# A state-space mixer with an MLP gate: the first norm factors and two exponentials move from ScalarE to GpSimd, GELU's table is loaded first, and the work is put in another order

## The chip, the core and the metric

The kernel runs on one core of one Trainium2 chip. A core has a matrix engine (TensorE, PE in the profile; its weight loads are PEld) and three engines for elementwise work: VectorE (DVE), ScalarE (ACT) and GpSimd (POOL). SyncE (SP) issues most transfers; ScalarE and GpSimd can issue transfers from queues of their own. Each engine works through its own list of instructions in order, and waits on semaphores where an instruction needs what another engine makes. The metric is the device time of one execution, in microseconds (us).

## The reference

One input x of 2048 rows and 448 columns is normalised (the mean taken off, divided by the root of the variance). Two branches work on the normalised xn, and their product is added to x:

```python
xn = _layernorm(x, axis=-1)
# A: a linear recurrence over the rows, with 448 complex states
dt = jnp.exp(log_dt); Lam_bar = jnp.exp(dt * Lam)
B_bar = ((Lam_bar - 1.0) / Lam)[:, None] * Bmat
h = Lam_bar[None, :] * h + Bu[:, t, :]                  # for every row t
s = 2.0 * jnp.einsum("blp,dp->bld", hseq, Cmat).real + xn * Dskip
# B: an MLP on a second normalisation of xn, 448 -> 1792 -> 448
hid = _gelu(_layernorm(xn) @ w1 + b1)
g = _silu(hid @ w2 + b2)
out = x + s * g
```

Inputs and outputs are bf16. Lam is the complex vector Lambda, Bmat and Cmat are complex matrices.

## The kernel before, in words

The 2048 rows are four groups (0 to 3) of 512. A group has two blocks (b = 0, 1) of 256 rows, and of each block the even and the odd rows (par = 0, 1) are one tile of 128 rows and 448 columns. Rows lie on partitions. `x_all` holds x, `xn_sb` and `xn2_sb` the once and twice normalised rows, `xnT` and `xn2T` their transposes, which TensorE needs as operands. The later transposes are made by transfers; those of the first group's `xn2T` are made on TensorE (`first_apply`, line 460), and their results are copied out of PSUM at line 464 (the profile shows the helper's line, 417).

The MLP of a group has a first layer (`mm1_run`, line 801, matmuls over pairs j of 128 hidden columns, each pair in two phases, then GELU on ScalarE, line 805) and a second layer (`mm2`, line 828, 14 matmuls to a tile, then an eviction with the bias on VectorE, line 831, and SiLU or tanh on ScalarE). w1 has 448 rows: three transfers' worth of 128 and a rest of 64, which `ldw1` loads with a transfer of its own for each of four column chunks (lines 347 and 348, keys `w1_c` and `w1r_c`) and copies to a second place (line 352, `w1c_c`), so that two 64-row matmuls can run side by side.

The recurrence branch needs parameters first. `parameters()` turns the three vectors Lambda_re, Lambda_im and log_dt into columns with small matmuls (line 529), takes exp(log_dt) and exp(dt Lambda_re) (lines 533 and 541) and a sine and cosine of the angles by range reduction and a polynomial (lines 552 to 555, `wrap` and `sine`). `tables` builds rotation tables (lines 624 to 640), `lb` and `bt` the input matrix (lines 659 to 661, then transposes by transfer), `cq` the output matrices CQ and CZ, `m0` a direct term M0. Then, for every group, input matmuls (`bu`, line 729), the scan (`ssm`) and output matmuls (`ym`, lines 871 to 877), a product with the gate and a sum with x (lines 885 to 896).

The first group's statistics are read by `first_stats` (lines 431 and 432). The factor 1/sqrt(variance) is made on ScalarE: Ln, then Exp of minus a half (lines 434 and 435 for the two tiles of block 0, 438 and 439 for both tiles of block 1 at once). Ln and Exp share an activation table (`natural_log_exp_and_others`, loaded at line 314), GELU needs another, which `gelu_table` loads (line 443) once the last of these factors and of the exponentials is made. `ln_scale` (lines 478 to 488) makes later factors either on GpSimd by the power operation or on VectorE by Newton steps.

All of this is written down as tasks, numbered as they are created. A task names its engine, or two engines of which the list `SECOND` picks the second. The list `ORDER` is the order in which the tasks are given out; each engine gets its own tasks in that order and works through them in that order. Waits follow from what a task reads and writes. So the two lists set, for each queue, what stands behind what.

Until the first MLP matmul, TensorE runs filler matmuls (`dummies`, line 422) between the small ones. The order of the first tasks before the change is, on ScalarE: three loads of vectors, the first table, Ln and Exp of block 0, the parameter columns, exp(log_dt), two copies of transposes, Ln and Exp of block 1, the second exponential, the GELU table, GELUs. On VectorE: statistics and aggregate of one tile, then of the other, each followed soon by its normalising; the bias copy, the copies of w1, block 1. On SyncE: x of block 0 and 1, the w1 chunks with their rests, x of blocks 2 and 3, w2, the matrices.

## Time and profile before

| | us |
|---|---|
| median of 3 runs | 153.37 (153.15 to 153.41) |
| span of the profiled execution, first to last instruction | 151.8 |
| the runs' median less that span | 1.6 |
| first MLP matmul starts | 6.85 |
| last matmul ends | 148.91 |

| engine | busy us | share of the span |
|---|---|---|
| TensorE | 147.1 | 97% |
| VectorE | 127.6 | 84% |
| ScalarE | 99.0 | 65% |
| GpSimd | 42.1 | 28% |

The profile is one execution. Its rows give a start, a length, the engine, the line of the kernel, the operation, the output and the inputs with their shapes, and in brackets how long the engine was idle just before and whose work ended that wait. Matmuls are pipelined, so that a busy TensorE need not be at its peak. Lengths on GpSimd are rough.

### The profile page before, as it was taken

To read this page: it belongs to the slowest core of one execution; us is meant where nothing else is said; L and a number is where in the kernel's file an instruction comes from. 1 tells how busy PE (TensorE), PEld (TensorE's weight loads), DVE (VectorE), ACT (ScalarE), POOL (GpSimd) and SP (SyncE) were. 2 spreads that over 40 slices of the span, in tenths; PEclk is the share of its full clock that TensorE was granted. 3 is DMA by queue.
4 is the path that set the end of the run, shared out by engine and by line. 5 is a ranking of instruction groups with operands and counts; after the bars stand their busy time and mean duration, and the time that the engine had idled before them with its cause. 6 is when DMAs were issued, how large, how long until landed. Compare 5 with 4: busy or idle time off the path is not lost.

```text
span 151.8 us, 2974 instructions
## 1 busy us (share of the span) xinstructions
PE 147.1 (97%) x1127; PEld 86.6 (57%) x1127; DVE 127.6 (84%) x267; ACT 99.0 (65%) x183; POOL 42.1 (28%) x101
## 2 busy tenths in 40 slices
PE   7899999999999999999999999999999999999992
PEld 7785755454566577545444556764454666555551
DVE  2874999999978979999999996379968726999984
ACT  3888996988789559997898610463579834067400
POOL 5376827153020920010456006200072031000201
PEclk9999999999999999999999999999999999999999
DMA  4999999989997300700003032610331001100022
GB/s 116 262 305 390 266 202 138 219 152 133 165 261 180 65 0 0 138 0 4 0 0 63 4 60 45 154 60 4 60 101 23 0 4 57 64 0 0 4 84 98
DMA packets 31236, 14.73 MB, mean 97 GB/s; under 512 B 24752, under 2 KB 30774, under 8 KB 31222
## 3 DMA queue, kind: packets, MB, share of 16 engines
q1 hardware_dynamic: 30912, 14.26, 41.8%
q0 software_dynamic: 160, 0.23, 1.0%
q8 instruction: 9, 0.15, 0.4%
q10 hardware_dynamic: 150, 0.05, 0.1%
q14 instruction: 5, 0.04, 0.1%
HBM read 6.89 MB, written 1.84 MB: 57 GB/s over the span
## 4 chain that ended last, share of the span: by engine, by line
PE 80%; DVE 9%; DMA 4%; SPq 4%; issue 2%
PE psum L828 23%; PE psum L801 22%; PE psum L729 14%; PE psum L871 13%; DMA x_all<-in_A_x_dram 4%; PE psum L874 4%; SPq L84 4%; PE psum L712 3%; DVE xn_sb L499 2%; DVE lnst L399 1%; DVE s_w L628 1%; PE psum L877 1%; DVE o L831 1%; PE psum L697 1%; DVE tmp L891 1%
## 5 line engine op out<-in xcount | busy, mean ns | idle before, releaser
L801 PE MATMUL psum<-xn2T,w_sb 64*128 64x512 bf16 (+1 forms) x462 | 44.6, 345 | 0.3 <-ACT xn2T L417 0.2
L828 PE MATMUL psum<-w_sb,gT 128*128 128x448 bf16 x224 | 44.5, 353 | 0.2 <-DVE o L831 0.2
L805 ACT ACTIVATE gT<-psum,b1f 128x512 bf16<-128x512 f32 (+1 forms) x66 | 35.9, 625 | 10.4 <-PE psum L801 10.2
L801 PEld LDWEIGHTS psum<-xn2T,w_sb 64*128 64x128 bf16 x462 | 24.1, 109 | 19.8 <-ACT gT L805 2.3
L828 PEld LDWEIGHTS psum<-w_sb,gT 128*128 128x128 bf16 x224 | 21.5, 98 | 20.7 <-DVE o L831 0.6
L417 ACT ACTIVATE u_sb<-psum 128x512 bf16<-128x512 f32 (+2 forms) x22 | 10.5, 478 | 23.0 <-PE psum L729 22.7
L729 PE MATMUL psum<-xnT,BT 128*128 128x256 bf16 x196 | 24.0, 273 | 0.0
L729 PEld LDWEIGHTS psum<-xnT,BT 128*128 128x128 bf16 x196 | 18.9, 98 | 5.4 <-issue 1.1
L891 POOL TENSOR_TENSOR tmp<-t,x_all 128x448 bf16<-128x448 bf16 x5 | 5.2, 1032 | 33.1 <-DVE t L888 30.7
L753 DVE TENSOR_TENSOR_SCAN s_w<-dk,vs 128x774 f32<-128x774 f32 x8 | 14.0, 1760 | 0.1
L500 ACT ACTIVATE xn_sb<-x_all,lnw 128x448 bf16<-128x448 bf16 (+2 forms) x21 | 13.0, 662 | 1.2 <-DVE xn_sb L499 1.1
L417 ACT ACTIVATE vs<-s_w 64x256 bf16<-64x256 f32 (+2 forms) x16 | 10.9, 681 | 2.6 <-DVE s_w L753 1.5
L871 PE MATMUL psum<-CZ,h_sb 128*128 128x448 bf16 x56 | 11.9, 352 | 0.0
L871 PE MATMUL psum<-CQ,h_sb 128*128 128x448 bf16 (+2 forms) x54 | 10.5, 332 | 0.0
L399 DVE BATCH_NORM_STATS2 lnst<-x_all 128x6 f32<-128x448 bf16 x12 | 7.1, 617 | 3.4 <-DMA x_all<-in_A_x_dram 3.4
L831 DVE TENSOR_TENSOR o<-psum,b2bc 128x448 f32<-128x448 f32 x16 | 9.7, 614 | 0.2
L871 PEld LDWEIGHTS psum<-CZ,h_sb 128*128 128x128 bf16 x56 | 5.4, 98 | 4.7 <-DVE lnmv L405 0.4
L871 PEld LDWEIGHTS psum<-CQ,h_sb 128*128 128x128 bf16 x54 | 5.1, 98 | 4.0 <-DVE t L885 0.4
L874 PE MATMUL psum<-M,xnT 128*128 128x448 bf16 x32 | 7.4, 352 | 0.0
L480 POOL TENSOR_TENSOR lnw<-lnw,mhalf 128x8 f32<-128x8 f32 x3 | 7.2, 2404 | 0.3
L883 DVE TENSOR_TENSOR Cr<-psum,xd 128x448 f32<-128x448 f32 x7 | 4.3, 620 | 3.5 <-PE psum L877 3.4
L499 DVE TENSOR_SCALAR xn_sb<-x_all,lnw 128x448 bf16<-128x448 bf16 (+2 forms) x19 | 6.9, 396 | 0.0
(160 smaller groups left out, 189.1 us busy)
## 6 DMA issues: line engine op xcount, KB each, us to landing
out_dram<-tmp SPq DMA_DIRECT2D x7, 224.0 KB, 2.0
x_all<-in_A_x_dram SPq DMA_DIRECT2D x3, 448.0 KB, 4.0
w_sb<-in_B_w_dram SPq DMA_DIRECT2D x3, 448.0 KB, 8.4
w_sb<-in_B_w_dram SPq DMA_DIRECT2D x3, 384.0 KB, 4.8
vs<-in_A_C_re_dram SPq DMA_DIRECT2D x1, 392.0 KB, 11.6
Bn<-in_A_B_im_dram SPq DMA_DIRECT2D x1, 336.0 KB, 10.2
Bn<-in_A_B_re_dram SPq DMA_DIRECT2D x1, 336.0 KB, 10.5
vs<-in_A_C_im_dram SPq DMA_DIRECT2D x1, 336.0 KB, 10.8
```

Source lines behind the costliest of these rows:

```text
L399: dve([lambda e, b=b, par=par, q=q: e.bn_stats(lnst[:, q, :], x_all[:, 2 * g + b, par, :])], [f"x{2 * g + b}"] , [f"st{q}"], 0.62, prio)
L417: kb.either(("act", [lambda e, o=o, i=i: e.activation(o, i, ACT.Copy) for o, i in pairs]), ("dve", [lambda e, o=o, i=i: e.tensor_copy(o, i ...
L499: on = [("dve", [lambda e, o=o, i=i: e.tensor_scalar(o, i, rs, nb, op0=ALU.mult, op1=ALU.add) for o, i in parts], 0.4, 0.12), ("act", [lam ...
L500: ("act", [lambda e, o=o, i=i: e.activation(o, i, ACT.Identity, bias=nb, scale=rs) for o, i in parts], 0.75, 0.2)]
L729: fns = [lambda e, r=r, m=m, d=d: e.matmul(psum[:, 4, r * NK:(r + 1) * NK], BT[:, m, d, :], xnT[:, gx, d, :], start=(d == 0), stop=(d == 6 ...
L753: dve(lambda e, so=so, vi=vi: e.tensor_tensor_scan(so, dk[:].rearrange("p i c -> p (i c)"), vi, 0.0, ALU.mult, ALU.add), ["v", "vl", "dk", ...
L801: return lambda e: e.matmul(view(bk[k]), w1_sb[rows, d, fcol(2 * j + k)], rhs[rows, d, :, :], start=not second and n == 0, stop=second and ...
L805: act([lambda e, k=k: e.activation(gT[:, gb, 2 * j + k, :].rearrange("p (r c) -> p r c", r=2)[:, :, cols], view(bk[k]), ACT.Gelu_apprx_tan ...
L828: fns = [lambda e, fi=fi: e.matmul(psum[:, bk, 0:D], gT[:, gb, fi, q * 128:(q + 1) * 128], w2_sb[:, fi, :], start=(fi == 0), stop=(fi == N ...
L831: dve(lambda e: e.tensor_tensor(o2[:, fb, :], psum[:, bk, 0:D], b2bc[:], ALU.add), [f"ps{bk}", "b2bc"], [f"oo{fb}"], 0.62, prio - 76)
L871: fns = [lambda e, k=k: e.matmul(psum[:, bk, c0:c1], h_sb[:, hb, k, k0:k0 + 128], cm[:, k, c0:c1], start=(k == 0), stop=False) for k in ra ...
L874: fns += [lambda e, d=d: e.matmul(psum[:, bk, c0:c1], xnT[:, gx, d, xs], M0[:, d, c0:c1], start=False, stop=(d == 3)) for d in range(4)]
```

## The change

The factors of the first normalisation are no longer made by Ln and Exp. A linear step makes (1 + eps) var + eps^2 on VectorE, and GpSimd raises it to the power of minus a half. Both exponentials become powers of e on GpSimd. As ScalarE then needs neither Ln nor Exp, its first table is GELU's, loaded near the start, and the later load is gone. The rests of w1 are loaded from ScalarE's queue. The copy of the transposes of block 0, par 0 is made in two halves. `ORDER` and `SECOND` are new throughout.

```diff
-            act(lambda e: e.preload_act_table_set("natural_log_exp_and_others"), [], ["warm"], 0.05, 5 * PINNED, "exp")
+            kb._sem("gelu0")
+            kb.add("act", lambda e: e.preload_act_table_set("gelu_apprx_tanh_and_others"), [], ["Wg0"], sem="gelu0")
...
+            pool(lambda e: e.memset(euler[:], math.e), [], ["euler"])
...
-                ld("sp", w1_sb[64:128, 3, a:a + w], dram_ap(B_w1, 384 * F + a, [[F, 64], [1, w]]), [f"w1r_{c}" for c in cs], 64 * w * 2, prio)
+                ld("act", w1_sb[64:128, 3, a:a + w], dram_ap(B_w1, 384 * F + a, [[F, 64], [1, w]]), [f"w1r_{c}" for c in cs], 64 * w * 2, prio)
...
+                    w1 = lnw[:, 0, 1, 1, q:q + 1]
                     if b == 0:
-                        kb.add("act", [lambda e, var=var, r1=r1: e.activation(r1, var, ACT.Ln, scale=1.0 + LN_EPS, bias=eps[:, 1:2]),
-                                       lambda e, r1=r1: e.activation(r1, r1, ACT.Exp, scale=-0.5)], [f"mv0_{q}", "eps", "warm"], [f"r1{q}"], chain=True)
+                        small(lambda e, var=var, w1=w1: e.tensor_scalar(w1, var, 1.0 + LN_EPS, LN_EPS * LN_EPS, op0=ALU.mult, op1=ALU.add), [f"mv0_{q}"], [f"w1{q}"])
+                        pool(lambda e, w1=w1, r1=r1: e.tensor_tensor(r1, w1, mhalf[:, 0, :], ALU.pow), [f"w1{q}", "mhalf"], [f"r1{q}"])
                     elif par == 1:
-                        vs2, rs2 = lnmv[:, 0, 1:4:2, 1], lnw[:, 0, 2, 1, 1:4:2]
...
+                        vs2, ws2, rs2 = lnmv[:, 0, 1:4:2, 1], lnw[:, 0, 1, 1, 1:4:2], lnw[:, 0, 2, 1, 1:4:2]
+                        small(lambda e: e.tensor_scalar(ws2, vs2, 1.0 + LN_EPS, LN_EPS * LN_EPS, op0=ALU.mult, op1=ALU.add), ["mv0_1", "mv0_3"], ["w11"])
+                        pool(lambda e: e.tensor_tensor(rs2, ws2, mhalf[:, 0, :].to_broadcast([128, 2]), ALU.pow), ["w11", "mhalf"], ["r11", "r13"])
...
-                    copy([(oap, psh[:, bank, 0:512].rearrange("p (d c) -> p d c", d=4))], [f"ps{bank}"], [f"xmT{b}p{par}"])
+                    for h in (0, 2) if b == 0 and par == 0 else (0,):
+                        n = 2 if b == 0 and par == 0 else 4
+                        copy([(oap[:, h:h + n, :], psh[:, bank, h * 128:(h + n) * 128].rearrange("p (d c) -> p d c", d=n))], [f"ps{bank}"], [f"xmT{b}p{par}" + "b" * (h > 0)])
...
-                act(lambda e: e.activation(col(DT), col(LDT), ACT.Exp), ["cp", "warm"], ["cdt"], 0.2, 3 * PINNED - 4, "exp")
+                pool(lambda e: e.tensor_tensor(col(DT), euler[:].to_broadcast([128, 4]), col(LDT), ALU.pow), ["cp", "euler"], ["cdt"])
...
-                act(lambda e: e.activation(col(R1), col(A1), ACT.Exp), ["ca"], ["cr"], 0.2, 3 * PINNED - 1, "exp")
+                pool(lambda e: e.tensor_tensor(col(R1), euler[:].to_broadcast([128, 4]), col(A1), ALU.pow), ["ca", "euler"], ["cr"])
...
-            gelu_table()
```

What the new `ORDER` and `SECOND` put where, read off the two lists (names of the tasks by what they make):

| engine | the first tasks after the change, in order |
|---|---|
| ScalarE | two vectors' loads, w1 rest 1, Lambda_re, w1 rest 0, GELU table, parameter columns, w1 rest 2, both half copies of block 0 par 0, w1 copies 1 and 0, bias copy, w1 rest 3, first GELU, Abs of the angles, second and third GELU, w1 copy 3, GELUs |
| GpSimd | constants and bias loads, power of block 0 par 0, of par 1, exp(log_dt), three small products, power of block 1, second exponential, `ln_scale` |
| VectorE | both statistics of block 0, both aggregates, both linear steps, statistic of block 1, both normalisings, statistic of block 1, copy of block 0 par 1, angle steps and aggregates, linear step of block 1, wrap, w1 copy 2, block 1's normalisings, two table steps, block 1's copies, sine, group 1's statistics, tables |
| SyncE | x of blocks 0 and 1, w1 chunks 1, 0, 2, 3, x of blocks 2 and 3, w2, matrices |
| TensorE | 26 filler matmuls, the parameters, 8 and 3 filler, both transposes of block 0 (before: 3 of the filler between the two); six second-layer matmuls among the last phases of the first layer; the first M0 matmuls right after the second input product, ahead of the third and of a second-layer tile; at the very end the 192-column piece of the last tile ahead of the 256-column piece (before: after it) |

Moved between engines further: `sine` and `wrap` from GpSimd to VectorE, the absolute value of `tables` (line 630) from VectorE to ScalarE, the bias copy and three of four copies of w1 from VectorE to ScalarE, one copy of block 0's transposes from ScalarE to VectorE.

12 lines of the change are left out of this document (4 added, 8 removed), and 34 rows, old and new, of the table ORDER.

## The prediction

> **What bounds the kernel now.** I read the page first (TensorE is busy almost throughout and carries most of the chain of waits), then the busy time by stretches, because an average over 151.8 us says nothing about where a microsecond can be won. Columns: stretch, its length, busy time (instructions) of PE, PEld, DVE, ACT and POOL, granted clock, DMA share, GB/s.
>
> ```profile
> 6.85:19.03 12.18, 12.05 (x176) 8.90 (x177) 8.89 (x32) 11.03 (x26) 8.73 (x26) 1.00 1.07 315
> 19.03:27.33 8.30, 8.12 (x45) 4.03 (x43) 8.02 (x28) 6.89 (x13) 3.89 (x13) 1.00 1.14 175
> 27.33:148.40 121.07, 121.07 (x847) 68.67 (x848) 105.53 (x195) 77.21 (x137) 25.44 (x46) 1.00 0.31 66
> 148.40:151.80 3.40, 0.51 (x7) 0.28 (x4) 1.41 (x4) 0.00 (x0) 0.75 (x1) 0.98 0.22 68
> ```
>
> From 27.33 to 148.40 TensorE is never idle and the clock is whole. So the change can win only ahead of 27.33 or in the 3.4 us tail, and it can lose anywhere, since every new gap on TensorE adds in full. The first microseconds, from the timeline (start, length, engine, line, operation):
>
> ```profile
> 1.61 0.27 ACTq L84 DMA_DIRECT2D dk<-in_A_Lambda_re_dram  x1
> ...
> 2.89 0.63 DVE L431 BATCH_NORM_STATS2 lnst<-x_all 128x6 f32<-128x448 bf16 x1 [1.85 <-DMA x_all<-in_A_x_dram]
> ...
> 3.56 0.18 DVE L432 BATCH_NORM_AGGREGATE lnmv<-lnst 128x2 f32<-128x6 f32 x1
> ...
> 3.65 0.59 DVE L431 BATCH_NORM_STATS2 lnst<-x_all 128x6 f32<-128x448 bf16 x1
> ...
> 3.83 0.29 ACT L434 ACTIVATE lnw<-lnmv,eps 128x1 f32<-128x1 f32 x1 [0.63 <-DVE lnmv L432]
> ...
> 4.03 0.21 PE L529 MATMUL psum<-ident,dk 3*128 3x3 bf16 x3 [0.27 <-DMA dk<-in_A_Lambda_re_dram]
> ...
> 4.15 0.20 ACT L435 ACTIVATE lnw<-lnw 128x1 f32<-128x1 f32 x1
> ...
> 4.32 0.87 PE L422 MATMUL psum<-const-bfloat16-1.0 128*128 128x128 bf16 x8
> ...
> 4.39 0.40 DVE L453 TENSOR_SCALAR xn_sb<-x_all,lnmv,lnw 128x448 bf16<-128x448 bf16 x1
> ...
> 5.45 1.25 ACT L417 ACTIVATE xn2T<-psum 128x512 bf16<-128x512 bf16 x2
> ...
> 6.85 2.50 PE L801 MATMUL psum<-xn2T,w_sb 64*128 64x256 bf16 x42 [0.19 <-ACT xn2T L417]
> ...
> 7.29 1.28 ACT L443 ACT_TABLE_LOAD   x1
> ...
> 7.51 0.70 DVE L453 TENSOR_SCALAR xn_sb<-x_all,lnmv,lnw 128x448 bf16<-128x448 bf16 x2
> ...
> 8.67 2.30 ACT L805 ACTIVATE gT<-psum,b1f 128x256 bf16<-128x256 f32 x6
> ...
> 9.28 0.62 PE L460 MATMUL psum<-ident,xn_sb 128*128 128x128 bf16 x8
> ...
> 9.84 9.26 PE L801 MATMUL psum<-xn2T,w_sb 64*128 64x256 bf16 x126
> ```
>
> The reader is to see a chain: the first rows of x land (2.89), statistics, Ln and Exp on ScalarE (0.52 us from 3.83 to 4.35), normalising, transposes, two ScalarE copies to 6.70, first MLP matmul at 6.85. Then the 126 matmuls from 9.84 are paced by GELU: ScalarE works 11.03 of 12.18 us. The third place is where VectorE and ScalarE have little in hand:
>
> ```profile
> 19.37 2.30 ACT L805 ACTIVATE gT<-psum,b1f 128x256 bf16<-128x256 f32 x6
> ...
> 22.77 0.62 DVE L831 TENSOR_TENSOR o<-psum,b2bc 128x448 f32<-128x448 f32 x1
> ...
> 24.29 1.23 DVE L631 SCALAR_TENSOR_TENSOR s_w<-s_w 128x1024 f32<-128x1024 f32 x1
> ...
> 27.33 2.82 PE L828 MATMUL psum<-w_sb,gT 128*128 128x448 bf16 x14 [0.18 <-DVE o L831]
> ...
> 30.08 10.11 PE L801 MATMUL psum<-xn2T,w_sb 64*128 64x512 bf16 x90
> ...
> 31.57 1.28 ACT L618 ACT_TABLE_LOAD   x1
> ...
> 32.94 3.58 ACT L805 ACTIVATE gT<-psum,b1f 128x512 bf16<-128x512 f32 x6
> ...
> 46.96 0.68 DVE L661 SCALAR_TENSOR_TENSOR CQ<-Cr,cw,tmp 128x448 bf16<-128x448 bf16 x1
> ...
> 48.46 1.49 PE L712 MATMUL psum<-CQ,Bn 128*128 128x448 bf16 x7
> ```
>
> **The change part by part.** Its operations on the chip:
>
> ```profile
> 2.19 4.53 SPq L84 DMA_DIRECT2D w_sb<-in_B_w_dram  x8
> ...
> 5.42 0.26 POOL L540 TENSOR_TENSOR cw<-cw 128x4 f32<-128x4 f32 x1 [2.55 <-ACT cw L533]
> ...
> 6.90 0.43 DVE L352 COPY w_sb<-w_sb 64x512 bf16<-64x512 bf16 x2
> ...
> 9.30 1.90 POOL L480 TENSOR_TENSOR lnw<-lnw,mhalf 128x8 f32<-128x8 f32 x1
> ...
> 11.27 0.21 POOL L481 TENSOR_TENSOR lnw<-lnmv,lnw 128x8 f32<-128x8 f32 x1
> ...
> 14.30 0.21 POOL L545 TENSOR_SCALAR ang<-ang 128x16 f32<-128x16 f32 x1
> ...
> 17.95 0.22 POOL L551 TENSOR_TENSOR ang<-ang 128x16 f32<-128x16 f32 x1
> ```
>
> *Power.* A product over 8 columns takes 0.21 us, a power over 8 takes 1.90. One column was never run: it lies between 0.21 and 1.90. I take 0.2 + 1/8 of the 1.7 difference, 0.4 us, since the extra is most simply work per element; four columns 1.05.
>
> *First factors.* Now both statistics run first (to 4.24), two aggregates and two linear steps of 0.18 follow, starts 0.1 apart: the first power starts at about 4.75 and ends at 5.15, the second at 5.6. Normalising ends at 5.6 and 6.0, where before it ended at 4.79 and 5.6. The parameter matmul waits for Lambda_re, whose issue (1.61) now stands behind one w1 load on ScalarE's queue (4.53/8 = 0.57 us): 4.03 becomes about 4.7, and with the 8 and 3 filler matmuls behind it TensorE is free for transposes at 6.1. The halved copy is two of some 0.4 us (1.25/2 = 0.63 whole; between 0.63 and 0.83 for both) on ScalarE; the other copy moves to VectorE behind a 0.6 us statistic and ends at 7.2. First MLP matmul about 7.4, later by 0.55.
>
> *ScalarE until the first GELU.* Removed: three Ln/Exp pairs (0.49 each), two Exps (0.2 each), one of two table loads (1.28), one copy (0.63): 3.8 us. Added: four DMA issues (up to 0.57 each, 2.3), three w1 copies taken from VectorE (at most 0.63 each by the copy row), the bias copy 0.2, the second half copy 0.2. It comes out even: after the copies at 7.3 stand two w1 copies (to 8.3), the bias copy and a DMA issue, and the first GELU starts at about 9.0 against 8.67. SyncE's x2/x3 issue comes 2 us earlier, but its data wait behind a DMA share of 1.07, and VectorE no longer reaches them before about 13.9; I count nothing.
>
> *The second half of the block.* Its factors now stand on VectorE behind the angle steps, which wait for the exp of log_dt, third power on GpSimd (6.7). Normalising it ends near 10.3 instead of 8.21 (7.51+0.70), so the transposes move from 9.28-9.90 to about 10.65. ScalarE's Abs stands between its first and second GELU and waits for the wrapped angle until 9.3. From 9.98 ScalarE runs without a gap: counting GELUs, one w1 copy and two normalisings in order, the last first-layer GELU ends at 21.8 (before: 19.37+2.30 = 21.67). But six second-layer matmuls (1.1 us) now stand among the last phases and fill a wait. MLP phases and those six are done at 20.2; before, 9.84+9.26 to 19.03 and six more give 20.17. Term A: 0.0, between -0.7 (no wait inside the phases) and +1.
>
> *Sine on VectorE.* Ten steps that GpSimd did between 14.30 and 18.17 take 2.0 us in VectorE's order (0.2 each, start to start), beside the wrap 0.6 and the linear steps 0.5; VectorE is rid of the 1.23 us absolute value (now ScalarE's), three w1 copies and the bias copy (1.1). Its former waits (it works 8.89 us of the 12.18) fill up. Adding its durations in order, the first eviction of the second layer ends near 25.05; TensorE wants that bank at 24.4. Wait 0.5 in place of today's 0.18. Term B: +0.3 (0 to +1.5).
>
> *ScalarE before group 1.* Three pieces more stand between the last GELU of the first layer and the table load at 31.57: the absolute value (1.2), one product and one normalising (0.65 each, by the copy row), 2.5 us. Of ScalarE's waits there (8.30 less 6.89, 1.4 us) a part stays, since the evictions that it waits for come later too. The GELUs of group 1 so start at 34.0 to 34.8 instead of 32.94, and the first pair (3.58/3) ends at 35.2 to 36.0. TensorE wants it after 42 matmuls of 0.11 (10.11/90), from 30.4 on: at 35.1. A wait of 0.1 to 0.9 for the first pair, and each later pair is paced by ScalarE again. Term C: +0.6 (0 to +1.6).
>
> *M0 earlier.* The new order puts the first M0 matmuls ahead of 14 second-layer (2.8 us by the row at 27.33) and 14 input matmuls (1.5), so they want CQ some 4.2 us sooner than 48.46; VectorE has three statistics fewer ahead of CQ (0.6 each) and, by its durations in order, finishes it at about 45 to 46 instead of 47.64. Term D: +0.2 (0 to +1.5).
>
> *Tail.*
>
> ```profile
> 147.70 1.09 DVE L885 SCALAR_TENSOR_TENSOR t<-psum,g_sb 128x448 bf16<-128x448 f32 x2 [0.31 <-PE psum L874]
> ...
> 149.01 0.35 DVE L885 SCALAR_TENSOR_TENSOR t<-psum,g_sb 128x192 bf16<-128x192 f32 x1
> ...
> 149.40 0.44 DVE L891 TENSOR_TENSOR tmp<-t,Cr 128x192 bf16<-128x192 bf16 x1
> ...
> 149.87 0.39 ACTq L84 DMA_DIRECT2D out_dram<-tmp  x1
> ```
>
> The last piece is now 256 columns wide, not 192: 0.08 and 0.1 more on VectorE by width, and SyncE's issue in place of ScalarE's. Term E: +0.25 (+0.1 to +0.4).
>
> Sum: 0.0 + 0.3 + 0.6 + 0.2 + 0.25 = +1.35 us. The profiled execution spans 151.8 us; the median 153.37 is 1.6 more, which I leave as it is. 151.8 + 1.35 + 1.6 = 154.7.
>
> The switch to GELU held ScalarE for 1.4 us here (7.29 to 8.67). The Trainium skill, ScalarE: Activation LUTs, What ACT_TABLE_LOAD costs, counts about 2.66 us for a switch, load and drain. By it ScalarE would win 1.3 us more and the sum would be near +0.1; the trace shows no drain of that kind, so I keep 1.4.
>
> **The rivals.** *Faster.* GELU is ready when its bank is, the six filling matmuls close the waits in the first layer, and TensorE runs packed from 7.4: A is -0.7, B to D nothing, E +0.25: 152.9; with the first matmul at 7.1 it is 152.6. For it: TensorE needs only about 11.1 of the 12.18 us. Against it: the Abs and the late second half stand in between. It decides if one power is at most 0.4 us and VectorE's first eviction ends by 24.4.
>
> *Power has a fixed price.* At 1.9 us whatever the width, the second factor is ready at 8.55, and the first matmul at about 9.85, 3.0 late, which the fill cannot return; B to D lie hidden in it: 156.4. For it: 1.90 is the only measured size.
>
> *Even.* The change does not do what it says on the path: ScalarE's savings go into its DMA issues and copies, A to D cancel, E stays: 153.6.
>
> *GpSimd must load code first.* The power is now GpSimd's first two-tensor operation, and a load there would stand on the start. The rows speak against it: 5.42 was such a first operation, took 0.26 and followed its input at once; it would need more than 3 us to show over the other terms, so 158 or more. The Trainium skill, GPSIMD Engine Reference, Instruction dispatch, has about 6 us for the first call of a freshly loaded kernel; by it the time would be near 160.
>
> **How the numbers follow.** Chances: forecast 0.49, faster 0.24, fixed price 0.17, even 0.08, code load 0.02. 0.2% is 0.3 us, about what a measurement of this kernel tells from no change. Slower 0.68, same 0.08, faster 0.24. The range 152.6 to 157.0 takes in the faster and the fixed-price case and the bounds of the terms, taken not all at once; the forecast's own is 153.7 to 156.2.
>
> **What would show it.** Right: a one-column power of about 0.4 us; first MLP matmul at 7.2-7.6; first GELU near 9; transposes of the second half after 10; a TensorE wait on the first eviction near 25, one on GELU near 35, one on CQ near 45; a tail of 3.6. Wrong: the stretch 27-148 without a gap and the second layer begun earlier; or powers of 1.9 us at the start.

## The result and the profile after

| | before | after |
|---|---|---|
| median, us | 153.39 (153.15 to 153.68, 4 runs) | 157.47 (157.33 to 157.62, 4 runs) |
| span of the profiled execution | 151.8 | 155.5 |
| first MLP matmul | 6.85 | 8.11 |
| first GELU | 8.67 | 10.51 |
| group 1's first matmul | 30.08 | 32.12 |

After over before is 1.0271, with a 95% interval of 1.0255 to 1.0288: 4.1 us slower, where 1.35 was forecast, and 0.5 us beyond the range. Ratios, here and below, compare means and leave out an execution that is over 1.5% above the fastest of its kernel (160.38 us in run 1, 156.36 in run 15). The timeline of TensorE in the kernel after (start, length, engine, line, operation, and in brackets the idle time before it with its releaser; line 803 is line 801 of before, 830 is 828, 731 is 729):

```profile
4.74 0.21 PE L531 MATMUL psum<-ident,dk 3*128 3x3 bf16 x3 [0.97 <-DMA dk<-in_A_Lambda_re_dram]
...
6.26 1.04 PE L460 MATMUL psum<-ident,xn_sb 128*128 128x128 bf16 x8
...
8.11 3.48 PE L803 MATMUL psum<-xn2T,w_sb 64*128 64x256 bf16 x42
11.52 0.62 PE L460 MATMUL psum<-ident,xn_sb 128*128 128x128 bf16 x8
12.07 1.28 PE L803 MATMUL psum<-xn2T,w_sb 64*128 64x256 bf16 x20
13.78 5.51 PE L803 MATMUL psum<-xn2T,w_sb 64*128 64x512 bf16 x70 [0.42 <-DVE ang L552]
19.22 1.31 PE L830 MATMUL psum<-w_sb,gT 128*128 128x448 bf16 x6
...
22.55 9.63 PE L830 MATMUL psum<-w_sb,gT 128*128 128x448 bf16 x50
32.12 5.37 PE L803 MATMUL psum<-xn2T,w_sb 64*128 64x512 bf16 x48
37.69 2.57 PE L803 MATMUL psum<-xn2T,w_sb 64*128 64x512 bf16 x22 [0.21 <-ACT gT L807]
...
55.85 1.69 PE L731 MATMUL psum<-xnT,BT 128*128 128x256 bf16 x14 [0.25 <-ACT u_sb L420]
...
59.13 1.70 PE L731 MATMUL psum<-xnT,BT 128*128 128x256 bf16 x14 [0.26 <-ACT u_sb L420]
...
70.63 1.70 PE L803 MATMUL psum<-xn2T,w_sb 64*128 64x512 bf16 x14 [0.39 <-DVE M L707]
```

The waits in brackets add up to 2.5 us, less than the 3.7 us by which the span grew. To see where these come in, take the moments at which TensorE has done the same set of tasks in both profiles, and the start of its next matmul there:

| at | before | after | late by |
|---|---|---|---|
| the parameters' matmuls | 4.03 | 4.74 | 0.71 |
| the first MLP matmul | 6.85 | 8.11 | 1.26 |
| 26 MLP matmuls done | 8.28 | 10.54 | 2.26 |
| in the second half of the first layer | 11.09 | 13.78 | 2.69 |
| group 1's first matmul | 30.08 | 32.12 | 2.04 |
| before the input matmuls at 53.20 | 53.20 | 55.85 | 2.65 |
| an M0 product later | 56.05 | 59.13 | 3.08 |
| in group 2's first layer | 72.78 | 76.53 | 3.75 |

So there are two places: the first 14 us cost 2.7 us, of which 0.65 come back until group 1, and the stretch from 53 to 71 us costs 1.5 us more (0.2 us go to GELU between the two, at 37.69). Behind 70.63 TensorE is never idle again, and the tail is as long as before. The busy times by stretches (columns as in the prediction):

```profile
70.63:152.11 81.48, 81.48 (x548) 45.43 (x549) 65.25 (x110) 35.40 (x61) 12.50 (x13) 1.00 0.13 33
152.11:155.51 3.40, 0.52 (x5) 0.21 (x3) 1.37 (x4) 0.00 (x0) 0.62 (x1) 1.00 0.36 117
```

The start, from the timelines of the other engines of the kernel after:

```profile
4.64 1.12 POOL L439 TENSOR_TENSOR lnw<-lnw,mhalf 128x1 f32<-128x1 f32 x2 [0.52 <-DVE lnw L438]
5.14 0.47 ACTq L84 DMA_DIRECT2D w_sb<-in_B_w_dram  x1
5.28 0.63 DVE L434 BATCH_NORM_STATS2 lnst<-x_all 128x6 f32<-128x448 bf16 x1 [0.79 <-DMA x_all<-in_A_x_dram]
5.73 1.01 POOL L535 TENSOR_TENSOR cw<-euler,cw 128x4 f32<-128x4 f32 x1
5.82 0.69 DVE L453 TENSOR_SCALAR xn_sb<-x_all,lnmv,lnw 128x448 bf16<-128x448 bf16 x2
7.67 0.50 ACTq L84 DMA_DIRECT2D w_sb<-in_B_w_dram  x1
8.74 0.76 POOL L443 TENSOR_TENSOR lnw<-lnw,mhalf 128x2 f32<-128x2 f32 x1 [1.23 <-DVE lnw L442]
10.51 0.84 ACT L807 ACTIVATE gT<-psum,b1f 128x256 bf16<-128x256 f32 x2 [1.92 <-PE psum L803]
```

The powers are not far from their estimates (0.56 us for one column, where 0.4 was estimated, and 1.01 for four, where it was 1.05). What was not in the forecast is the length of the matmuls. The groups by shape, first the kernel after from 8.1 to 10.3 us, then the kernel before from 6.85 to 9.2 us (count, busy us, mean ns of one):

```profile
L803 PE MATMUL psum<-xn2T,w_sb 64*128 64x256 bf16 x22 | 2.4, 398 | 0.1
```

```profile
L801 PE MATMUL psum<-xn2T,w_sb 64*128 64x256 bf16 x42 | 2.5, 270 | 0.2 <-ACT xn2T L417 0.2
```

The same matmuls, with no wait between them, come at about half the pace (22 in 2.4 us against 42 in 2.5). That is the 1.0 us between the second and the third row of the table, and no wait shows it. The stretches give the granted clock (the share of TensorE's full clock) as 1.00 in both kernels, but they count as 1.00 the time ahead of the first entry in the trace's record of the clock. That entry, full clock, stands at 4.88 us in the kernel before and at 10.21 in the kernel after, and the pace changes there: in the kernel before the fillers start 107 ns apart until 4.83 us and 60 ns apart from 4.91; in the kernel after the slow matmuls end at 10.2. So TensorE begins at half pace in both kernels, and the change put off its full clock by 5.3 us.

### The profile page after: what moved, and what is told of

Its sections match the earlier page's. It is cut to its first block, busy times and chain, and to the rows that moved or that the text cites. A ratio compares the mean times of both kernels' runs of the same rounds, so it can differ in the third digit from the quotient of the medians.

```text
span 155.5 us, 2976 instructions
## 1 busy us (share of the span) xinstructions
PE 149.1 (96%) x1127; PEld 88.6 (57%) x1127; DVE 128.8 (83%) x293; ACT 94.4 (61%) x174; POOL 39.4 (25%) x85
## 4 chain that ended last, share of the span: by engine, by line
PE 61%; DVE 15%; ACT 15%; issue 3%; POOL 3%; DMA 2%; ACTq 1%; DVEq 0%
PE psum L803 18%; PE psum L830 15%; PE psum L873 13%; PE psum L731 8%; ACT xn_sb L502 4%; PE psum L876 4%; DVE tmp L661 3%; DVE Bn L663 3%; ACT gT L807 3%; DVE CQ L663 2%; ACT u_sb L420 2%; ACT tmp L660 2%; ACT vs L420 2%; DMA dk<-in_A_Lambda_re_dram 2%; DVE lnst L402 1%
## 5 line engine op out<-in xcount | busy, mean ns | idle before, releaser
L803 PE MATMUL psum<-xn2T,w_sb 64*128 64x512 bf16 (+1 forms) x462 | 45.7, 351 | 1.2 <-DVE ang L552 0.4
L807 ACT ACTIVATE gT<-psum,b1f 128x512 bf16<-128x512 f32 (+1 forms) x66 | 36.6, 623 | 7.8 <-PE psum L803 7.4
L803 PEld LDWEIGHTS psum<-xn2T,w_sb 64*128 64x128 bf16 x462 | 25.6, 110 | 20.4 <-issue 3.1
L420 ACT ACTIVATE u_sb<-psum 64x256 bf16<-64x256 f32 (+2 forms) x19 | 8.6, 455 | 14.9 <-PE psum L731 14.8
L502 ACT ACTIVATE xn_sb<-x_all,lnw 128x448 bf16<-128x448 bf16 (+2 forms) x19 | 11.9, 669 | 4.0 <-POOL xd L849 2.4
L420 ACT ACTIVATE vs<-s_w 64x256 bf16<-64x256 f32 (+2 forms) x13 | 9.7, 743 | 4.5 <-DVE s_w L755 4.4
L837 ACT ACTIVATE th<-o 128x448 f32<-128x448 f32 x8 | 4.6, 574 | 7.8 <-DVE o L833 7.7
L420 DVE CAST u_sb<-psum 128x512 bf16<-128x512 f32 x5 | 3.4, 689 | 5.8 <-PE psum L731 5.8
L849 POOL TENSOR_TENSOR xd<-xn_sb,dbc 128x448 bf16<-128x448 bf16 x2 | 3.9, 1950 | 13.3 <-DVE Cr L885 13.3
L835 ACT ACTIVATE g_sb<-o 128x448 bf16<-128x448 f32 x8 | 4.5, 569 | 4.4 <-DVE o L833 4.3
```

Of the source, the lines that this page charges most:

```text
L420: kb.either(("act", [lambda e, o=o, i=i: e.activation(o, i, ACT.Copy) for o, i in pairs]), ("dve", [lambda e, o=o, i=i: e.tensor_copy(o, i ...
L502: ("act", [lambda e, o=o, i=i: e.activation(o, i, ACT.Identity, bias=nb, scale=rs) for o, i in parts], 0.75, 0.2)]
L803: return lambda e: e.matmul(view(bk[k]), w1_sb[rows, d, fcol(2 * j + k)], rhs[rows, d, :, :], start=not second and n == 0, stop=second and ...
L807: act([lambda e, k=k: e.activation(gT[:, gb, 2 * j + k, :].rearrange("p (r c) -> p r c", r=2)[:, :, cols], view(bk[k]), ACT.Gelu_apprx_tan ...
```

## The experiments

On the chips of these runs the kernel before took 153.3 to 153.4 us (medians; single executions 153.1 to 155.3). The ratio is to the kernel before on the same chip.

| kernel | median us (lowest to highest, runs) | over before, 95% interval |
|---|---|---|
| 1 after, 36 fillers | 158.58 (157.75 to 160.38, 4) | 1.0289, 1.0209 to 1.0368 |
| 2 after, w1's rests on SyncE | 156.79 (155.76 to 157.27, 4) | 1.0181, 1.0109 to 1.0254 |
| 3 after, late order of before | 156.59 (156.43 to 157.05, 4) | 1.0182, 1.0118 to 1.0246 |
| 4 before, 16 fillers | 155.01 (154.46 to 155.87, 10) | 1.0096, 1.0063 to 1.0128 |
| 5 after, start mended | 156.32 (155.56 to 156.96, 4) | 1.0184, 1.0131 to 1.0236 |
| 6 the same, late order of before | 154.18 (154.00 to 155.27, 10) | 1.0048, 1.0019 to 1.0077 |
| 7 before, w1's rests on ScalarE's queue | 155.99 (155.64 to 156.63, 4) | 1.0169, 1.0119 to 1.0219 |
| 8 before, middle order of after | 155.72 (155.27 to 157.16, 6) | 1.0158, 1.0106 to 1.0210 |
| 9 as 6, two ScalarE tasks back | 155.16 (155.05 to 156.81, 6) | 1.0128, 1.0087 to 1.0169 |
| 10 as 6, product for power | 154.40 (153.88 to 155.95, 7) | 1.0072, 1.0035 to 1.0110 |
| 11 as 9, product for power | 155.09 (154.86 to 155.64, 4) | 1.0109, 1.0071 to 1.0146 |
| 12 as 6, fewer fillers | 154.90 (153.83 to 156.00, 10) | 1.0078, 1.0039 to 1.0117 |
| 13 as 6, order before group 1 | 154.02 (153.69 to 155.04, 12) | 1.0022, 0.9990 to 1.0055 |
| 14 after, one statistic later | 158.18 (157.63 to 158.39, 4) | 1.0285, 1.0236 to 1.0334 |
| 15 as 13, one statistic later | 154.10 (153.97 to 156.36, 12) | 1.0041, 1.0012 to 1.0069 |
| 16 after again | 158.03 (157.60 to 158.72, 4) | 1.0292, 1.0245 to 1.0338 |

**1. More fillers in the kernel after.**

```diff
-            dummies(26)
+            dummies(36)
```

> The kernel after with 36 filler matmuls instead of 26 behind the first transposes, nothing else. In the trace of the kernel after, TensorE stands still from 3.76 to 4.74 us (before: 0.27 us), and its first 22 matmuls of the first MLP layer then take 398 ns each where the same matmuls before took 270 ns, though the granted clock reads 1.00 in both. Theory C (that gap made TensorE slow for some microseconds): with the gap filled they take about 270 ns, first group's delay falls by about 1 us, and the time goes from 157.4 to about 156.4 us (155.9 to 156.8). Rival (the matmuls are slow for another reason, such as waiting for operands): they stay near 400 ns and the time stays within 157.1 to 157.8.

TensorE's timeline in its profile:

```profile
8.04 2.50 PE L803 MATMUL psum<-xn2T,w_sb 64*128 64x256 bf16 x42
10.48 0.62 PE L460 MATMUL psum<-ident,xn_sb 128*128 128x128 bf16 x8
11.65 1.28 PE L803 MATMUL psum<-xn2T,w_sb 64*128 64x256 bf16 x20 [0.55 <-DMA w_sb<-in_B_w_dram]
15.22 7.19 PE L803 MATMUL psum<-xn2T,w_sb 64*128 64x512 bf16 x70 [2.30 <-DMA w_sb<-in_B_w_dram]
```

In this execution, the one at 160.38 us, the matmuls were quick (42 in 2.50 us), the second transposes came 1.04 us sooner than in the kernel after (10.48 against 11.52), and then TensorE waited 2.85 us for w1's rests; it went on at 15.22, in the kernel after at 13.78. The time did not fall: the other three executions took 157.75 to 158.69, the unchanged kernel in run 16 157.60 to 158.72. So theory C held for the matmuls and failed for the time: in this profile the quick matmuls only reach the late rests sooner. In this execution TensorE paid a second time, by the stretches:

```profile
16.00:20.00 4.00, 4.00 (x34) 2.54 (x31) 3.80 (x20) 2.10 (x4) 2.26 (x9) 0.57 1.15 235
```

Behind the wait the granted clock averages 0.57 over 16 to 20 us; the record has it at half from 16.45 to 19.86. A long wait can thus cost more than its length.

**2. The rests of w1 back on SyncE's queue.** In `ORDER` each of the four loads stands right behind the chunk that it completes.

```diff
-                ld("act", w1_sb[64:128, 3, a:a + w], dram_ap(B_w1, 384 * F + a, [[F, 64], [1, w]]), [f"w1r_{c}" for c in cs], 64 * w * 2, prio)
+                ld("sp", w1_sb[64:128, 3, a:a + w], dram_ap(B_w1, 384 * F + a, [[F, 64], [1, w]]), [f"w1r_{c}" for c in cs], 64 * w * 2, prio)
```

> The kernel after with the four loads of w1's last 64 rows put back on SyncE's queue, each right behind the chunk it completes; nothing else. ScalarE's queue then holds only the small loads, so Lambda_re is issued earlier. Theory Q (the loads on ScalarE's queue delay the parameters and land late): Lambda_re's matmul starts about 0.5 us earlier than 4.74, the wait of 0.42 us at 13.78 is gone, and the time falls by 0.4 to 0.9 us to 156.5 to 157.0; if the shorter gap also keeps TensorE quick (270 ns instead of 398 ns), by up to 1.9 us to 155.5. Rival (the powers alone set the delay): first MLP matmul stays at 8.1 and the time within 157.1 to 157.8.

Lambda_re's matmul started at 3.69, 1.05 us sooner, the wait at 13.78 was gone (its row names VectorE's angles, which these matmuls do not read), and the median fell by 0.7 us, from 1.0271 to 1.0181 of before. The matmuls stayed slow (groups by shape, 7.6 to 9.9 us):

```profile
L809 PE MATMUL psum<-xn2T,w_sb 64*128 64x256 bf16 x22 | 2.5, 413 | 0.1
```

There was now no gap before the parameters, only one of 0.36 us before the transposes, and the matmuls were slow all the same, until the clock record's first entry at 10.10; run 12, whose instructions are the same until group 1, shows them quick. The opposite edit is run 7.

**3. The late order of before.** From group 1's first matmul on, `ORDER` and `SECOND` are those of before.

```diff
-ORDER, SECOND: as in the kernel after throughout
+ORDER, SECOND: as after up to group 1's first matmul, then the remaining tasks as before
```

> The kernel after until the first matmul of group 1's MLP (TensorE 2.04 us late there), and from there on the order of tasks and the second choices of engine of the kernel before. Theory L (the new order behind that point costs by itself: TensorE's delay grows from 2.24 at 53 us to 3.08 at 59 us and 3.75 at 70.6 us, at waits behind GpSimd's and ScalarE's tasks): the delay stays near 2.0 and the time is about 155.6 (155.2 to 156.1). Rival (those waits follow from the late start whatever the order): delay grows as before and the time stays at 157.0 to 157.8.

The waits at 55.85, 59.13 and 70.63 are gone, and behind group 1's first layer TensorE is not idle. Against the kernel after the profile's delay goes from +1.28 us at 37.7 to -0.20 at 76.5, that is 1.5 us won in the late stretch. The median won only 0.9 (156.59, where 155.2 to 156.1 was expected); in the profiled execution the start was later by 0.4 us at the first MLP matmul (8.53) and the matmuls slow for longer, until 12.8 us. The late order costs by itself.

**4. Fewer fillers in the kernel before.**

```diff
-            dummies(26)
+            dummies(16)
```

> The kernel before with 16 filler matmuls instead of 26 behind the first transposes; nothing else. TensorE then stands still for about a microsecond before the parameters' matmuls, as in the kernel after. Theory C (such a gap makes TensorE slow for some microseconds): the first matmuls of the MLP take about 400 ns instead of 270 and the time rises by 0.5 to 1.2 us, to 153.9 to 154.6. Rival (the gap costs nothing because nobody waits for the fillers): 153.2 to 153.6, the same.

1.6 us slower (0.5 to 1.2 expected), by taking away work that nobody waits for. The parameters' matmul even came 0.59 us sooner (3.44 against 4.03), behind a gap of 0.75 us; the second row of x was read later (4.09 against 3.65), and the first MLP matmul came at 7.49, 0.64 us late. From the timeline and by shape from 7.4 to 9.8 us:

```profile
3.44 0.21 PE L529 MATMUL psum<-ident,dk 3*128 3x3 bf16 x3 [0.75 <-DMA dk<-in_A_Lambda_re_dram]
```

```profile
L801 PE MATMUL psum<-xn2T,w_sb 64*128 64x256 bf16 x23 | 2.6, 408 | 0.3 <-ACT xn2T L417 0.3
```

The clock record's first entry stands at 9.94 (before: 4.88), and until then TensorE's delay grows by 1.1 us to 1.8. So theory C's price is shown for the kernel before, though not as it says it: a gap ahead of the first MLP matmul does not slow TensorE, it puts off the full clock.

**5 and 6. The start mended, then the late order as well.**

```diff
-            dummies(8, ["vr0"])
+            dummies(14, ["vr0"])
...
-                            dummies(2, ["xm0p0"])
+                            dummies(6, ["xm0p0"])
```

together with the edit of run 2; in run 6 also that of run 3.

> The kernel after with w1's last 64 rows on SyncE's queue again and 10 more fillers: 14 instead of 8 behind the parameters and 6 instead of 2 between the first two sets of transposes, so that TensorE has no gap of more than 0.2 us before the first MLP matmul; the powers, the table load, the halved copy and the order stay. Theory CQ (TensorE slow after gaps, and the late rests of w1, each hide the other: with 36 fillers alone the matmuls took 270 ns but then waited 0.55 and 2.30 us for the rests; with the rests alone moved they took 418 ns and nothing waited): first MLP matmul at about 7.65 us, 270 ns each, no wait for w1; the time falls from 157.4 to 155.0 to 155.8. Rival (it is the chain of powers that counts, the rest is noise of a start): 156.5 to 157.5.

> The same as the run with the mended start, and from group 1's first matmul on the order and second choices of the kernel before. What is left of the change are the powers, the table load in front, the halved copy and the order until there. Theory CQL (three causes that add: slow TensorE 1.0 to 1.4, rests of w1 0.4 and more, late order 1.2): 153.6 to 154.4, so that the powers themselves cost 0.3 to 1.0 us. Rival (the powers' delay of the first matmul of 0.8 us goes through the whole kernel): 154.5 to 155.5.

Run 5 lies between the two expectations: the matmuls were quick, nothing waited for w1, TensorE was 0.28 us late at group 1's first matmul (30.36) and 1.6 us later in the end than in run 6, by the spans. Run 6 came out as expected, 0.8 us above before. TensorE and ScalarE in its profile:

```profile
7.67 2.50 PE L810 MATMUL psum<-xn2T,w_sb 64*128 64x256 bf16 x42
...
30.09 5.66 PE L810 MATMUL psum<-xn2T,w_sb 64*128 64x512 bf16 x48
36.07 4.77 PE L810 MATMUL psum<-xn2T,w_sb 64*128 64x512 bf16 x42 [0.32 <-ACT gT L814]
```

```profile
31.16 0.58 ACT L842 ACTIVATE g_sb<-o 128x448 bf16<-128x448 f32 x1 [0.43 <-DVE o L840]
31.64 0.49 ACT L649 ACTIVATE WT<-s_w,sgn 128x256 bf16<-128x256 f32 x1
32.22 1.28 ACT L627 ACT_TABLE_LOAD   x1
```

From 7.67 to 30.09 are 22.42 us, before 23.23: the change does win 0.8 us in group 0's MLP, as much as its start loses. Then the second load of the GELU table comes 0.65 us later than before (31.57), and TensorE loses 0.65 us to GELU at 34 to 36 us. That is all that is left in this profile.

**7. The rests alone, in the kernel before.** The line of run 2 the other way round, with the four issues at the places that the kernel after has.

> The kernel before with only the four loads of w1's last 64 rows moved to ScalarE's queue, at the places that they have in the kernel after. Theory Q (this part is enough to make it slower): Lambda_re lands about 0.5 us later, at 4.5, TensorE stands still for about 0.8 us before it and is slow for its first matmuls or, where it isn't, waits 1 to 3 us for the last rest, which lands 6 to 7 us behind an issue at 6.5 to 7.5; the time is 154.4 to 156.4. Rival (these 224 KB are hidden beside the large loads): 153.2 to 153.7.

2.6 us slower from this part alone. TensorE was 1.6 us late at the first MLP matmul (8.48) and 3.05 when the full clock came (11.50). TensorE's timeline and its groups by shape (8.4 to 10.8 us):

```profile
5.21 0.22 PE L535 MATMUL psum<-ident,dk 3*128 3x3 bf16 x3 [1.44 <-DMA dk<-in_A_Lambda_re_dram]
```

```profile
L807 PE MATMUL psum<-xn2T,w_sb 64*128 64x256 bf16 x23 | 2.7, 412 | 0.3 <-ACT xn2T L423 0.3
```

Lambda_re came 1.2 us later than before, though its issue stands behind one more transfer only (0.54 us). SyncE's queue, rid of the four rests, has issued the four large chunks of w1 by 4.49 us (with the rests by 6.72 before), and then issues the 448 KB of x's blocks 2 and 3, in run 7 (first two rows) against before (last):

```profile
2.20 2.29 SPq L84 DMA_DIRECT2D w_sb<-in_B_w_dram  x4
4.53 0.49 SPq L84 DMA_DIRECT2D x_all<-in_A_x_dram  x1
```

```profile
6.77 0.59 SPq L84 DMA_DIRECT2D x_all<-in_A_x_dram  x1
```

So the small early transfers now meet more large ones; that this is what holds Lambda_re back is likely and was not tried by itself. The rests themselves land later too; from the list of transfers (size, median us to landing), in the kernel after and before:

```profile
w_sb<-in_B_w_dram ACTq DMA_DIRECT2D x3, 64.0 KB, 5.9
```

```profile
w_sb<-in_B_w_dram SPq DMA_DIRECT2D x3, 64.0 KB, 4.6
```

How much each of the two does was not separated. The Trainium skill, DMA: Bandwidth & Descriptors, Issuing engines are not separate DMA queues, says that a second issuing engine saves only the time of issuing, as all transfers share the same 16 engines. The landing times agree: 5.9 us from the second queue, 4.6 from the one.

**8. The middle order of after, in the kernel before.**

```diff
-ORDER, SECOND: as before throughout
+ORDER, SECOND: as before up to the second half's first transposes, as after up to group 1's first matmul, then as before
```

> The kernel before with the order and second choices of the kernel after between the second half's first transposes and group 1's first matmul, and nothing else of the change. In the trace of the kernel after TensorE's delay against before falls from 2.69 us at 13.8 to 2.04 at 32.1 us, of which the wait of 0.18 us on VectorE's eviction that is gone is a part. Theory M (the new order of the middle saves by itself): 0.2 to 0.6 us less than before, 152.8 to 153.2. Rival (only the slow start made that room): 153.2 to 153.8.

Inconclusive, and outside both ranges: with the two orders joined, the absolute value of the angles, which ScalarE takes between two GELUs, waited for VectorE, and TensorE for it, 1.74 us at 12.49. Without this wait group 1's first matmul would have come at about 31.76 less 1.74, 30.02, level with before; that is an estimate.

**9 to 11. ScalarE's load before group 1, and the powers.**

```diff
-SECOND: Abs of the tables on ScalarE; ORDER: one normalising of group 1 before the second GELU table
+SECOND: Abs of the tables on VectorE; ORDER: that normalising behind group 1's first matmuls
```

```diff
-                        pool(lambda e, w1=w1, r1=r1: e.tensor_tensor(r1, w1, mhalf[:, 0, :], ALU.pow), [f"w1{q}", "mhalf"], [f"r1{q}"])
+                        pool(lambda e, w1=w1, r1=r1: e.tensor_tensor(r1, w1, mhalf[:, 0, :], ALU.mult), [f"w1{q}", "mhalf"], [f"r1{q}"])
```

> The kernel of the run with the mended start and the late order of before, with two tasks taken from ScalarE's stretch between the two loads of the GELU table and put where the kernel before has them: Abs of the tables' angles on VectorE (1.07 us on ScalarE) and one normalising of group 1 behind group 1's first matmuls (0.76 us). In the profile with the mended start TensorE is level with before at group 1's first matmul (30.09 against 30.08 us), the second load of the GELU table starts at 32.22 us against 31.57, and TensorE then loses 0.65 us at 34 to 36 us to GELU. Theory S (the step C of the forecast: ScalarE's extra work before group 1 is what is left): the load starts at about 31.6, the loss is gone, and the time is 153.3 to 153.7, that of before. Rival (VectorE, now later with its evictions, takes ScalarE's place): 153.9 to 154.5.

> The kernel of the run with the mended start and the late order of before, with a product in the place of the first two powers, so that the first normalising uses a wrong factor (the power of the first block's two rows is left out; all else is computed). Theory S (behind a mended start ScalarE's stretch before group 1 is the bound, not the first normalising): the first MLP matmul comes 0.5 to 0.8 us earlier, at about 7.0, and the time stays at 153.9 to 154.3. Rival (the powers' delay goes through): 153.3 to 153.7.

> Both edits: ScalarE's two tasks back and a product in the place of the first two powers (whose power is left out). Theory S with an open bound: with ScalarE's stretch relieved, the earlier first MLP matmul is worth 0.2 to 0.7 us, 152.7 to 153.3, which is what the powers cost at most. Rival (a third resource, the evictions on VectorE, holds group 1's start): 153.3 to 153.7.

Theory S fell in run 9, whose 155.16 us lie above the rival's range too. Taking 1.83 us from ScalarE made the second load of the GELU table later, not earlier:

```profile
32.97 1.28 ACT L627 ACT_TABLE_LOAD   x1
```

ScalarE waits there for VectorE's evictions, and VectorE with 1.22 us more to do brings them later (the last at 31.27 against 30.52). In run 10 the two first factors took 0.33 us in place of 1.11, and the time did not move (154.40 against 154.18); in run 11 neither (155.09 against 155.16). The first MLP matmul of run 10's profile came at 7.55, not at 7.0, because VectorE waited 0.53 us for a row of x there; so its profile doesn't tell what an earlier start is worth, but the times of both pairs say that with a mended start the powers cost less than these runs can tell, about half a microsecond.

**12. The fillers once more, with all else mended.** The kernel of run 6 with the fillers of the kernel after.

```diff
-            dummies(14, ["vr0"])
+            dummies(8, ["vr0"])
...
-                            dummies(6, ["xm0p0"])
+                            dummies(2, ["xm0p0"])
```

> The kernel of the run with the mended start and the late order of before, with the fillers of the kernel after (26, 8, 3, 2) instead of 26, 14, 3, 6; nothing else. Theory C (gaps before the first MLP matmul leave TensorE slow for the next microseconds): the first 20 or more MLP matmuls take about 415 ns instead of 270 and the time rises by 0.8 to 1.6 us, to 155.0 to 155.8. Rival (fillers change nothing that counts): 154.0 to 154.4.

Its ten times lie in two groups: 153.83, 153.88, 153.91, 154.10, then 154.53, then 155.26, 155.33, 155.50 and twice 156.00. With the fillers nine of ten lay between 154.00 and 154.60 and one at 155.27. The profile is one of the first group (154.10), and its matmuls took 270 ns (42 of them from 7.39 us), where the same start in run 2's profile had 413:

```profile
L810 PE MATMUL psum<-xn2T,w_sb 64*128 64x256 bf16 x42 | 2.5, 270 | 0.2 <-DVE cw L549 0.2
```

So the same instructions start at either pace; the clock record's first entry stands at 5.44 us here and at 10.10 in run 2's profile. That the second group of times is the one with slow matmuls was not seen in a trace of this kernel; it fits their price of 1.0 to 1.4 us, and the three executions at 155.50 and 156.00 have a mean granted clock of 0.989, which is 3.4 us at half clock. The expectation named one time for all; it is rather that more fillers make the quick start likely. The means of runs 6 and 12 (1.0048 and 1.0078 of before) can't be told apart.

**13 to 16. What was still open.** Run 13 moves five tasks in run 6's order (names by what they make); run 14 moves one task of the kernel after, run 15 the same task in run 13.

```diff
-VectorE: LB1, dbc, LB4, xd, xd, eviction 3, tmp, tmp, eviction 4
-ScalarE: W, normalising, W, gate 3, gate 4, last W, GELU table
+VectorE: LB1, eviction 3, dbc, LB4, xd, xd, eviction 4, tmp, tmp
+ScalarE: W, gate 3, normalising, W, last W, gate 4, GELU table
```

```diff
-VectorE: statistics of block 1's first row, both normalisings of block 0
+VectorE: both normalisings of block 0, statistics of block 1's first row
```

> The kernel of the run with the mended start and the late order of before, with five tasks moved in the order ahead of group 1: VectorE's two last evictions of group 0 run as soon as their sums are there (the first at about 27.9 instead of 29.24 us, the second right behind the last second-layer matmul, at 30.15 instead of 30.52), with two scalings of 0.40 us behind them, and ScalarE's last 0.49 us of sines ahead of the last gate. Nothing is added or taken away. Theory S2 (the order in front of the second load of the GELU table is what costs the last 0.65 us, not the amount of ScalarE's work, which when moved to VectorE made it 1.4 us): the load starts at 31.3 to 31.7 instead of 32.22, TensorE loses nothing at 34 to 36 us, and the time is 153.2 to 153.7, that of before. Rival (it is the amount of work on ScalarE and VectorE together): 154.0 to 154.4.

> The kernel after with one task moved: the statistics of block 1's first row, for which VectorE waits 0.79 us until 5.28 us while block 0's first factor is there by about 5.2, come behind block 0's two normalisings. Theory V (this row of x holds the first normalising at 5.82): the first normalising starts at about 5.25, the first MLP matmul comes about 0.5 us earlier than 8.11, and the time falls by 0.3 to 0.6 us to 156.8 to 157.2, or by 1.5 where TensorE's clock comes up a window earlier. Rival (w1's late rests give it all back at 13.8 us): 157.3 to 157.7.

> The kernel with the tail's new order and, besides, block 1's first statistics behind block 0's normalisings as well. Theory: with group 1's start free of ScalarE's delay, an earlier start of the first MLP matmul (7.4 or less) is worth at most 0.3 us, 153.0 to 153.6; rival (the last eviction of group 0, which can't come before its matmul, holds the table load): same as with the tail's order alone, within 0.2 us.

> The kernel after once more, unchanged, on the chip of these runs, for the scatter of its start. Theory C (the clock comes up at a moment that the program does not set, so the same kernel has starts that differ by up to 1.7 us): times between 156 and 158 in more than one cluster. Rival (its start is the same each time): all within 0.3 us of 157.4.

Run 13 can't be told from before (interval 0.9990 to 1.0055), but nor, clearly, from run 6: its median is 0.7 us above before and 0.16 below run 6. In its profile the start was slower, and the table load stayed where it was:

```profile
32.21 1.28 ACT L627 ACT_TABLE_LOAD   x1
```

Group 1's first matmul came at 30.41 there, so the load stands 1.80 us behind it, against 2.13 in run 6 and 1.49 before: the order gave back half of the 0.65 us, and the time lies in the rival's range. What the other half is stays open. In run 14 the first normalising moved to 5.17 as theory V had it, but in its profile Lambda_re and the bias landed later still (waits of 1.16 and 0.37 us), the first MLP matmul came at 8.59, and the time was the same as the unchanged kernel's on that chip (158.18 against 158.03). Run 15 is level with run 13. These runs can tell no cost of VectorE's order at the start. Run 16 has two pairs, 157.60 and 157.66, 158.40 and 158.72, which is more scatter than the 157.33 to 157.62 of the first four runs, and in its profile the matmuls were slow (414 ns from 8.4 to 10.8 us; the clock record's first entry is at 11.74).

None of these kernels is faster than before.

## Why the prediction was wrong

The sign was right and the mechanism mostly not. Undone one after the other, the 4.1 us are, by medians: 1.15 the fillers and w1's rests (157.47 to 156.32; 1.7 from the 158.03 of run 16, on the chip of runs 5 and 6), 2.1 the late order (to 154.18; 1.6 by the two profiles' spans), and 0.8 what is left.

*Power, first factors.* 0.4 and 1.05 us were estimated, 0.56 and 1.01 measured; a power of two columns took 0.76. The steps behind it held to some tenths of a microsecond where the start was not disturbed: with w1's rests on SyncE's queue the first MLP matmul came at 7.39 to 8.00 (forecast 7.4), and in run 6 the first GELU at 9.09 (9.0) and the last first-layer GELU ended at 21.77 (21.8). The account of ScalarE calls 3.8 us removed and 4.6 added (four issues 2.3, three copies of 0.63, twice 0.2) even; it is so only without the third w1 copy, which stands behind the third GELU.

*Term A, put at 0.0: this is the step that failed.* The MLP phases and the six matmuls were done at 22.55 us, not at 20.2, so the term measured +2.4; the delay was 2.69 on the way and 2.04 at group 1's first matmul. Two things were left out. The DMA issues moved to ScalarE's queue were counted by the time that their issue takes, and of SyncE's earlier issue the prediction said "I count nothing"; but Lambda_re, a row of x and the rests landed later, and the move alone cost the kernel before 2.6 us (run 7), a longer gap ahead of the parameters included. And TensorE's idle time ahead of its first real matmul was taken as free, because nothing waited for the fillers: the row at 4.03 with its gap of 0.27 us was read as harmless, and the gap of about 1 us that followed from the forecast's own 4.7 was not priced. It put off TensorE's full clock from 4.88 to 10.21 us, and the half pace cost 1.0 us behind the first MLP matmul here and 1.1 in run 4. The two partly hid each other, so that run 1 alone won nothing.

*Term B, +0.3.* There was no wait on the first eviction, and the 0.18 us of before were gone; TensorE's delay fell by 0.35 us there.

*Term C, +0.6.* A later table load did cost TensorE 0.65 us in run 6, but that the size agrees is in part luck. The GELUs came 0.65 us later there (33.59 against 32.94), where 1.1 to 1.9 was forecast, and runs 9 and 13 show that the load hangs on VectorE's evictions and on the order as well, not on the pieces added to ScalarE alone. And the term was added where it should have been compared: with TensorE 2.04 us late at group 1 the GELUs were late on a TensorE that was later still, and the wait was 0.21 us.

*Term D, +0.2.* M0 did not wait for CQ. The new order lost 1.5 us in the same stretch at places that the forecast had not looked at. GpSimd and ScalarE in the kernel after:

```profile
48.86 1.99 POOL L482 TENSOR_TENSOR lnw<-lnw,mhalf 128x8 f32<-128x8 f32 x1
```

```profile
51.94 2.73 ACT L502 ACTIVATE xn_sb<-x_all,lnw 128x384 bf16<-128x384 bf16 x5 [1.42 <-POOL lnw L484]
```

A power of eight columns ends at 50.85, ScalarE waits 1.42 us for the factors and then normalises for 2.73 us, and behind it stand the copies of the input product that TensorE waits for at 55.85. Four more normalisings, from 55.74 to 58.13, stand ahead of the copy for 59.13. Run 3 shows that it is the order; which of the moved tasks it is was not tried.

*Term E, +0.25.* Nothing: the tail stretch is 3.40 us in both. On VectorE the 256 columns took 0.42 and 0.43 us, the 192 of before 0.35 and 0.44.

*The rivals.* Fixed price: no (0.56 us for one column). Code load on GpSimd: no, the first two powers took 1.12 us together. The 6 us that the Trainium skill, GPSIMD Engine Reference, Instruction dispatch, gives for a first call don't show. Even: no, the start alone cost 2 us and more. Faster: the gain in group 0's MLP that it counted on is there (0.8 us in run 6), but the start and the late order took more. The upper end of the range, 157.0, allowed for the fixed price of a power and not for a TensorE at half pace.

## What to carry to other kernels

In every kernel here TensorE begins at half pace, and idle moments ahead of its first real work put off the full clock: price the next few microseconds at half pace, even where nobody waits for what it was doing. When small loads move to another queue, look at what the old queue now issues sooner, and follow every small early transfer to its landing, not to its issue. Terms of a sum that lie one behind the other on different engines are to be compared, not added, and a new order is searched for waits over its whole length.

## What the runs showed of the hardware

TensorE's clock at the start: in all 17 profiles whose trace has a record of the clock (all but run 13's), TensorE runs at half pace until the record's first entry. Fillers start 107 ns apart before it and 60 behind it; 64x256 matmuls take 398 to 414 ns and come in pairs at half the rate before it, and 270 ns behind it. The record's stretches of full clock last 3, 41, 42, 43 or 44 times 3.413 us, and its one stretch of half clock within a kernel (run 1) lasts 3.413 us. So the clock changes at the ends of windows of 3.413 us. Counted back from the first entry, with TensorE's idle time in the windows (ends of matmuls are modelled):

| profile | full clock from, us | idle in the window that ends there | idle in the window before | first MLP matmul |
|---|---|---|---|---|
| before | 4.88 | 0.27 | 2.78 | 6.85 |
| after | 10.21 | 0.16 | 0.97 | 8.11 |
| run 1 | 6.21 | 0.00 | 1.45 | 8.04 |
| run 2 | 10.10 | 0.15 | 0.36 | 7.62 |
| run 4 | 9.94 | 0.28 | 0.84 | 7.49 |
| run 6 | 6.57 | 0.00 | 1.09 | 7.67 |
| run 7 | 11.50 | 0.28 | 0.53 | 8.48 |
| run 12 | 5.44 | 0.09 | 2.21 | 7.39 |
| run 16 | 11.74 | 0.13 | 0.28 | 8.46 |

In all 17, a window with at most 0.27 us of idle time brought the full clock and none with 0.36 or more did; from 0.28 to 0.30 both occur. Once granted, the full clock outlasted a window with 1.37 us of idle time (run 11), and was halved for one window behind one with 2.2 us (run 1). Where the windows lie differs between executions of the same instructions (runs 2 and 12; the kernel after and run 16), so the same start comes at either pace. The Trainium skill, TensorE: Matmul & The Clock Gate, What's actually happening, says that the array starts at half its clock, is let go after a busy window of some 3.4 us, and that these windows run free of the kernel's start. The traces agree, and show how much idle time such a window may hold. The scatter of before (153.1 to 155.3) may be the same thing; no trace shows it.

GpSimd's power on 128 rows: 0.56 us for one column, 0.76 for two, 1.01 to 1.13 for four, 1.65 to 2.0 for eight in the kernel after (1.90 to 3.05 before), so about 0.4 us and 0.15 to 0.2 for each column. A product of one column took 0.19 (run 10).
